# Complex products of the high tables: additions moved from VectorE to accumulating DMAs, cosine bias as a constant, half the DMA scratch

## The chip, the cores and the metric

The kernel runs on one core of a Trainium2 chip. The metric is the device time in microseconds of one execution, as a median over runs. The engines are named as in the profile: PE (TensorE matmuls) with PEld (its weight loads), DVE (VectorE), ACT (ScalarE), POOL (GpSimd) and SP (SyncE). SP, ACT and POOL can issue DMAs; those of POOL go through the software queue (q0 in the profile), those of SP and ACT through hardware queues (q1, q10).

## The reference, cut to what matters

The output joins two independent halves of 448 columns over 2048 positions, in bfloat16.

```
# half A: linear attention, 16 heads of 28
q, k, v = split(x @ wqkv)
phi(t)  = concat(softmax(t @ w_phi), softmax(-(t @ w_phi)))
o       = phi(q) @ (phi(k)^T v) / (phi(q) . sum phi(k) + 1e-6)
a       = o @ wo
# half B: state space convolution, 448 channels with 256 complex states each
dt = exp(log_dt);  A = A_re + i A_im;  B, C likewise
P[d, n, l] = exp(dt[d] A[d, n] l)              # l = 0 .. 2047, in bf16 steps
K[d, l]    = Re( sum_n C[d, n] dt[d] B[d, n] P[d, n, l] )
y          = causal convolution of u with K along l  +  u * Dskip
```

What matters here is K. The exponent is split as l = hi + lo. A table of C dt B exp(dt A hi) for 32 values of hi (the high table) and a table of exp(dt A lo) for 50 values of lo are multiplied and summed over the states by PE.

## The kernel before, in words

The 448 channels are cut into eight chunks of 56. States lie on the 128 partitions, in two halves, so that a chunk has COLS = 112 columns per table entry. For each chunk k these steps run:

- `dampings` and `rotations` (L733 to L744): PE forms the arguments in PSUM, ACT evaluates Exp into `E`, and Sin twice into `W`, once for the cosine (line L742, with pi/2 as bias) and once for the sine. Each `use` covers 224, 448 or 896 columns per instruction.
- `hi_tables` (L760): the high table `U[:, k % 2]`, 32 entries, each a real and an imaginary row of 112 columns. Entries 0 to 3 are copied from `H`; then five levels follow, each a complex product of earlier entries with a power from `PW` (128, 256, or 512 three times): entries 4-7 from 0-3, 8-15 from 0-7, 16-23 from every second one of 0-15, 24-27 from every second one of 16-23, and 28-31 from 24-27. Each level reads what the one before it wrote. The product itself is `cmul` (L605): four `tt` calls (L416 to L419) on DVE, with the scratch tile `t2`.
- `damp` (L746): DVE multiplies `W` by `E`; then the sign flip of line L757 runs on ACT (profile line L758) or DVE.
- `build_k` (L773): PE multiplies `U` by `W`, 112 small matmuls per half chunk, and a copy brings the result from PSUM into `Ts`.

`U`, `W` and `E` have two places, by the parity of k. Between the chunks the program places the key side of half A (`key_tile`, L794), its queries (`query`, L836), the spectrum of u (`signal_spectrum`, L672), and the scattering of K from `Ts` to rows of `Kt` by many small DMAs on SP, POOL and ACT (`scatter_k`, L896). After the chunks come the spectrum of K, `load_su` (L973, the spectrum of u back from DRAM), the products and the inverse transform (`conv_group`, L1015).

The order of the instructions is fixed when the program is built. `Plan` (L148) collects units of work; a unit has a cost per engine on which it may run, its reads and writes, and a rank by its step label. `Plan.run` (L214) walks a clock of its own: at each step it takes the engine that can start earliest and, among units that can start then, that of the lowest rank in `RANKS` (L105). A unit that may run on ACT or DVE goes to whichever is free first. For ACT steps with a table, `PHASES` (L141) is a second order: a phase of a higher number may not start while one of a lower number is left; even numbers are Exp, odd ones Sin. For a DMA, `dma` (L457) gives the cost of its issue and a time on the wires (`load`), from which `run` sets the moment from which readers may be placed. On the chip each engine then executes its own queue in order and waits on semaphores. All engines' working data lie in one SBUF tile, at byte offsets written out by hand (L471 on).

The four lines of the product before:

```
        tt(tmp, src, pw(1), ALU.mult)
        tt(dst, src, pw(0), ALU.mult)
        tt(d[0], d[0], t[1], ALU.subtract)
        tt(d[1], d[1], t[0], ALU.add)
```

Of the kernel before, what the change touches and what calls it, by code (L numbers as in the profile page):

```python
# [9 lines left out]
BF16 = mybir.dt.bfloat16  # L10
# [89 lines left out]
def pair_rows(x2, row, t, col):  # L100
# [4 lines left out]
RANKS = {"in": 76, "inAre": 129, "inAim": 160, "inCre": 137, "inBre": 274, "inCim": 272, "inBim": 280, "inx0": 84,  # L105
         "inx1": 209, "inx2": 217, "inx3": 227, "inqk": 141, "inG": 164, "inv_": 281, "one": 67, "pid": 139, "bd":
         124, "dt": 198, "stAre": 19, "stAim": 18, "amp": 265, "hl": 238, "cs128": 177, "cs32": 202, "cs64": 161,
         "stCre": 14, "stBre": 260, "stCim": 8, "stBim": 140, "cb": 230, "H32": 98, "H64": 35, "pw": 57, "xT0": 277,
         "xT1": 190, "xT2": 121, "xT3": 0, "fold1": 135, "fold0": 235, "vones": 49, "late0": 24, "late1": 259,
         "late2": 15, "zero": 206, "ua0.0": 147, "ab0.0": 136, "ua0.1": 143, "ab0.1": 59, "ua0.2": 123, "ab0.2": 148,  # L110
         "ua0.3": 252, "ab0.3": 88, "us0.0": 215, "us0.1": 3, "us0.2": 5, "us0.3": 30, "us0.4": 50, "us0.5": 219,
         "us0.6": 203, "us0.7": 48, "exps0": 271, "rot0": 70, "hi0.0": 42, "hi0.1": 192, "hi0.2": 46, "hi0.3": 105,
         "hi0.4": 263, "hi0.5": 196, "exps1": 257, "rot1": 183, "hi1.0": 34, "hi1.1": 81, "hi1.2": 37, "hi1.3": 110,
         "hi1.4": 158, "hi1.5": 261, "damp0": 233, "neg0": 207, "build0.0": 65, "build0.1": 255, "ua1.0": 131,
         "ab1.0": 269, "ua1.1": 16, "ab1.1": 226, "ua1.2": 248, "ab1.2": 106, "ua1.3": 78, "ab1.3": 182, "us1.0": 33,
         "us1.1": 166, "us1.2": 68, "us1.3": 262, "us1.4": 234, "us1.5": 97, "us1.6": 126, "us1.7": 1, "key0": 225,
         "key1": 80, "key2": 171, "key3": 239, "key4": 253, "key5": 167, "key6": 151, "key7": 91, "exps2": 276,
         "rot2": 77, "hi2.0": 178, "hi2.1": 61, "hi2.2": 29, "hi2.3": 279, "hi2.4": 231, "hi2.5": 111, "damp1": 211,
         "neg1": 107, "build1.0": 113, "build1.1": 28, "exps3": 201, "rot3": 208, "hi3.0": 267, "hi3.1": 174, "hi3.2":
         115, "hi3.3": 157, "hi3.4": 243, "hi3.5": 218, "damp2": 240, "neg2": 132, "build2.0": 138, "build2.1": 237,  # L120
         "key8": 216, "key9": 133, "key10": 118, "key11": 173, "key12": 89, "key13": 36, "key14": 116, "key15": 93,
         "keyend": 146, "exps4": 176, "rot4": 205, "hi4.0": 223, "hi4.1": 108, "hi4.2": 153, "hi4.3": 63, "hi4.4": 26,
         "hi4.5": 47, "damp3": 40, "neg3": 23, "build3.0": 128, "build3.1": 125, "kt5": 244, "sc0": 247, "exps5": 32,
         "rot5": 258, "hi5.0": 275, "hi5.1": 254, "hi5.2": 199, "hi5.3": 212, "hi5.4": 270, "hi5.5": 7, "damp4": 52,
         "neg4": 79, "build4.0": 200, "build4.1": 163, "qe0": 117, "qz0": 104, "q0.0": 112, "q0.1": 142, "q0.2": 222,
         "q0.3": 144, "qe1": 96, "qz1": 92, "q1.0": 11, "q1.1": 134, "q1.2": 31, "q1.3": 69, "exps6": 22, "rot6": 94,
         "hi6.0": 189, "hi6.1": 56, "hi6.2": 12, "hi6.3": 246, "hi6.4": 43, "hi6.5": 188, "damp5": 169, "neg5": 38,
         "build5.0": 159, "build5.1": 175, "sc1": 229, "exps7": 213, "rot7": 250, "hi7.0": 273, "hi7.1": 266, "hi7.2":
         85, "hi7.3": 102, "hi7.4": 120, "hi7.5": 165, "damp6": 75, "neg6": 64, "build6.0": 194, "build6.1": 181,
         "negid": 54, "gi": 101, "su0": 187, "qe2": 185, "qz2": 100, "q2.0": 152, "q2.1": 9, "q2.2": 21, "q2.3": 119,  # L130
         "qe3": 156, "qz3": 242, "q3.0": 25, "q3.1": 2, "q3.2": 122, "q3.3": 168, "f0.0": 45, "ks0.0.0": 27,
         "ks0.0.1": 55, "f0.1": 197, "ks0.1.0": 179, "ks0.1.1": 103, "f0.2": 145, "ks0.2.0": 149, "ks0.2.1": 245,
         "f0.3": 86, "ks0.3.0": 210, "ks0.3.1": 53, "f0.4": 264, "ks0.4.0": 214, "ks0.4.1": 71, "f0.5": 127,
         "ks0.5.0": 193, "ks0.5.1": 191, "f0.6": 249, "ks0.6.0": 17, "ks0.6.1": 114, "f0.7": 184, "ks0.7.0": 62,
         "ks0.7.1": 90, "damp7": 278, "neg7": 41, "build7.0": 51, "build7.1": 73, "ks1.3.0": 10, "ks1.3.1": 95,
# [231 lines left out]
def kernel(  # L367
# [62 lines left out]
    def act(out_, a, func, phase=None, scale=1.0, bias=None, n=None):  # L430
        kw = {} if bias is None else {"bias": bias}
        plan.add({"ACT": 0.055 + (n or count(out_)) * 0.833e-3 + (0.093 if bias is not None else 0)},
                 lambda: nc.scalar.activation(at(out_), at(a), func, scale=scale, **kw),  # L433
                 [whose(a)] + ([] if bias is None else [bias]), [out_], phase)
# [718 lines left out]
```

## Time and profile before

| | |
|---|---|
| time, median of 3 runs | 342.79 us (341.43 to 343.74) |
| profiled execution, span | 341.7 us (the page gives no time outside the span) |
| DVE busy | 309.2 us (90%), 438 instructions |
| PE busy | 266.8 us (78%) |
| ACT busy | 254.2 us (74%) |
| POOL busy | 54.3 us (16%), 99 instructions |
| ACT_TABLE_LOAD | 12, 1283 ns each |
| DMA | 32.88 MB, of it 4.26 MB on the software queue |

The profile is that of one execution. Busy time counts an engine's instructions without waits and without overlap; the mean duration of an instruction in a group can exceed its share of the busy time, where the next one starts before it ends. In a timeline or a chain, the columns are the start, the length of a merged piece, the engine, the line, the operation with output and input shapes (partitions x elements), and the count. A line is often that of a helper: L419 is every two-input DVE operation, L433 every activation, L443 every copy out of PSUM, L468 every DMA issue. In a group the numbers are busy us, mean ns of one, and the idle time just before with its releasers. In the list of DMAs the last number is the median time from issue to landing, which the profile gives for POOL's alone.

### The profile page before, as it was taken

How to read it: one execution, taken by the hardware profiler on the slowest of the kernel's cores; microseconds unless marked ns; L12 is line 12 of the kernel's file. 1: busy time of each engine (PE TensorE's matmuls, PEld its weight loads, DVE VectorE, ACT ScalarE, POOL GpSimd, SP SyncE). 2: the span in 40 equal slices, each digit the busy share in tenths (PEclk: the TensorE clock that was granted, in tenths of full speed). 3: DMA queues.
4: the chain of work that ended last, by engine and by line, in shares of the span. 5: the costliest groups of instructions: out<-in, count | busy, mean ns of one | idle time of the engine just before them, and what ended most of it. 6: DMA issues, size and time to landing. Idle time of an engine off the chain costs nothing. (4 is left out here: it accounts for less than half of the span.)

```text
span 341.7 us, 9894 instructions
## 1 busy us (share of the span) xinstructions
PE 266.8 (78%) x4193; PEld 210.5 (62%) x4193; DVE 309.2 (90%) x438; ACT 254.2 (74%) x466; POOL 54.3 (16%) x99
## 2 busy tenths in 40 slices
PE   2536767888585989879997869998987686959984
PEld 1435743554563854755686647787775366949984
DVE  0578999999999999998999899999997979999992
ACT  4789999995999996986899999999976112214330
POOL 2100000000000000000019500007920035910000
PEclk9965579999899999998989998999998769999999
DMA  6994111221001002100203210322539968533333
GB/s 165 236 325 102 25 54 59 82 81 54 19 30 39 31 2 82 56 2 2 84 2 28 51 57 19 109 81 12 146 95 351 352 173 166 157 112 89 102 108 111
DMA packets 31062, 32.88 MB, mean 96 GB/s; under 512 B 8603, under 2 KB 29596, under 8 KB 30634
## 3 DMA queue, kind: packets, MB, share of 16 engines
q1 hardware_dynamic: 24338, 26.79, 25.9%
q0 software_dynamic: 3568, 4.26, 5.8%
q10 hardware_dynamic: 3112, 1.19, 1.6%
q8 instruction: 33, 0.54, 0.7%
q14 instruction: 11, 0.09, 0.1%
HBM read 24.28 MB, written 7.34 MB: 93 GB/s over the span
## 5 line engine op out<-in xcount | busy, mean ns | idle before, releaser
L453 PEld LDWEIGHTS <-sbuf 128*32 128x32 bf16 (+5 forms) x4049 | 196.2, 122 | 105.3 <-issue 52.5
L419 DVE TENSOR_TENSOR sbuf<-sbuf 128x448 bf16<-128x448 bf16 (+8 forms) x291 | 239.2, 872 | 7.0 <-ACT sbuf L433 3.1
L453 PE MATMUL mm<-sbuf 128*32 128x50 bf16 (+8 forms) x2151 | 144.7, 280 | 24.7 <-DVE sbuf L419 5.7
L433 ACT ACTIVATE sbuf<-arg 128x448 bf16<-128x448 f32 (+3 forms) x152 | 89.5, 710 | 0.0
L453 PE MATMUL kb<-sbuf 128*32 128x50 bf16 (+8 forms) x1152 | 74.7, 255 | 15.3 <-DVE sbuf L419 9.6
L443 ACT CAST sbuf<-mm 128x448 bf16<-128x448 f32 (+3 forms) x71 | 41.5, 599 | 25.2 <-PE mm L453 15.6
L453 PE MATMUL arg<-sbuf 128*128 128x112 bf16 (+1 forms) x746 | 49.0, 224 | 12.2 <-ACT sbuf L433 6.8
L468 POOL DMA_DIRECT2D sbuf<-sbuf x75 | 42.4, 594 | 92.0 <-ACT sbuf L443 90.4
L433 ACT ACTIVATE sbuf<-arg,sbuf 128x448 bf16<-128x448 f32 (+2 forms) x64 | 47.2, 738 | 0.8 <-PE arg L453 0.7
L443 ACT CAST sbuf<-kb 128x448 bf16<-128x448 f32 (+4 forms) x38 | 21.4, 572 | 20.7 <-PE kb L453 17.8
L433 ACT ACTIVATE sbuf<-mm 128x448 bf16<-128x448 f32 (+1 forms) x58 | 30.4, 604 | 8.0 <-PE mm L453 7.7
L809 DVE TENSOR_REDUCE sbuf<-sbuf 128x32 f32<-128x896 bf16 x16 | 17.2, 1072 | 1.2 <-ACT sbuf L433 1.2
L433 ACT ACT_TABLE_LOAD x12 | 15.4, 1283 | 3.5 <-issue 3.3
L633 PE MATMUL kb<-sbuf 128*112 128x128 bf16 x64 | 8.7, 310 | 10.2 <-DMA sbuf<-in_A_x_dram 7.8
L443 DVE CAST sbuf<-mm 128x448 bf16<-128x448 f32 (+3 forms) x22 | 13.2, 609 | 2.4 <-PE mm L453 2.4
L443 ACT CAST sbuf<-arg 128x224 bf16<-128x224 f32 (+1 forms) x13 | 4.6, 391 | 13.8 <-PE arg L453 13.8
L633 PEld LDWEIGHTS <-sbuf 128*112 128x112 bf16 x64 | 7.8, 208 | 11.3 <-DMA sbuf<-in_A_x_dram 8.4
L758 ACT ACTIVATE sbuf<-sbuf 128x1680 bf16<-128x1680 bf16 x8 | 13.9, 1732 | 0.7 <-DVE sbuf L419 0.7
L443 DVE CAST sbuf<-kb 128x448 bf16<-128x448 f32 (+2 forms) x15 | 9.2, 618 | 3.6 <-PE kb L453 1.9
L433 ACT ACTIVATE sbuf<-sbuf 128x896 f32<-128x896 f32 (+1 forms) x11 | 11.8, 1115 | 0.0
L419 DVE TENSOR_TENSOR sbuf<-kb,sbuf 128x448 bf16<-128x448 f32 (+3 forms) x19 | 9.9, 544 | 1.9 <-PE kb L453 1.8
L419 DVE TENSOR_TENSOR sbuf<-mm,sbuf 128x448 bf16<-128x448 f32 (+1 forms) x21 | 11.3, 566 | 0.4 <-PE mm L453 0.4
(35 smaller groups left out, 81.1 us busy)
## 6 DMA issues: line engine op xcount, KB each, us to landing
sbuf<-const SPq DMA_DIRECT2D x36, 224.0 KB
SUd<-sbuf SPq DMA_DIRECT2D x16, 224.0 KB
sbuf<-const SPq DMA_DIRECT2D x3, 1024.0 KB
sbuf<-in_A_x_dram SPq DMA_DIRECT2D x4, 448.0 KB
out_dram<-sbuf SPq DMA_DIRECT2D x16, 112.0 KB
sbuf<-in_B_u_dram SPq DMA_DIRECT2D x4, 448.0 KB
sbuf<-SUd POOLq DMA_DIRECT2D x1, 1792.0 KB, 17.9
sbuf<-SUd POOLq DMA_DIRECT2D x2, 896.0 KB, 10.0
```

Source lines behind the costliest of these rows:

```text
L419: lambda: nc.vector.tensor_tensor(out=at(out_), in0=at(a), in1=at(b), op=op), [whose(a), whose(b)], [out_])
L433: lambda: nc.scalar.activation(at(out_), at(a), func, scale=scale, **kw),
L443: lambda e: (nc.scalar.copy if e == "ACT" else nc.vector.tensor_copy)(at(out_), at(a)), [whose(a)], [out_])
L453: nc.tensor.matmul(out_, lhsT=lhsT, rhs=rhs, start=start, stop=stop, **kw)
L468: plan.add({e: own[e] for e in engs}, lambda e=engs[0]: QUEUES[e].dma_start(out=out_, in_=in_), r, w, lat=lat, load=pieces / 16000 * max(2 ...
L633: mms(p, [lambda t, j=j, x=x: nc.tensor.transpose(t[:, j, :], x[:, 112 * j:112 * j + 112], ident[:, :]) for j in range(4)], 0.4, [x, ident ...
L758: lambda en: nc.scalar.mul(m, m, -1.0) if en == "ACT" else nc.vector.tensor_scalar_mul(m, m, -1.0), [m], [m])
L809: plan.add({"DVE": 0.98}, lambda: nc.vector.tensor_reduce(zk[:, :, :], EK[:, :, :].rearrange("p s (h f) -> p s h f", f=D_HEAD), axis=AX.X, ...
```

## The change

1. In `hi_tables` each level's product is written as two DVE multiplications and one DMA. The first multiplies the source, read with its real and imaginary halves swapped, by (-im, im) into `t2`. The second multiplies the source by the real part into the destination. Then a DMA issued from POOL adds `t2` to the destination, SBUF to SBUF, with the add operation of the DMA. The negated imaginary parts `nq` are made once per chunk, on ACT or DVE, for the three powers together. `t2` gets a tile per level, at three places in turn.
2. `dma` takes `add`, which passes the operation on and doubles the planned time on the wires. The planner takes 1.0 us for the issue of such a DMA.
3. The cosine's bias is the constant pi/2 instead of a column in SBUF; the DVE memset of that column is gone, and the planner counts 93 ns less for these activations.
4. The scratch in SBUF for descriptors of software DMAs is set to 8192 bytes per partition; no size was given before. The working tile grows from 212800 to 219584 bytes per partition, and some small tiles move.
5. `RANKS` and `PHASES` are new throughout.

`cmul` stays as it is for the two products `H32` and `H64` at the start. The diff, without `RANKS`, and of `PHASES` the last part:

```diff
-          18, "key14": 18, "key15": 20, "exps4": 24, "rot4": 23, "exps5": 22, "rot5": 27, "qe0": 18, "qe1": 20, "exps6":
-          34, "rot6": 35, "exps7": 28, "rot7": 35, "qe2": 28, "qe3": 28}
+         "exps4": 26, "rot4": 23, "exps5": 16, "rot5": 27, "qe0": 24, "qe1": 16, "exps6": 30, "rot6":
+         37, "exps7": 28, "rot7": 43, "qe2": 60, "qe3": 56}
...
-    sb = Bytes(sb_pool.tile([128, 212800 // 2], BF16, name="sbuf"))
+    sb = Bytes(sb_pool.tile([128, 219584 // 2], BF16, name="sbuf"))
...
-    def act(out_, a, func, phase=None, scale=1.0, bias=None, n=None):
-        kw = {} if bias is None else {"bias": bias}
-        plan.add({"ACT": 0.055 + (n or count(out_)) * 0.833e-3 + (0.093 if bias is not None else 0)},
-                 lambda: nc.scalar.activation(at(out_), at(a), func, scale=scale, **kw),
-                 [whose(a)] + ([] if bias is None else [bias]), [out_], phase)
+    def act(out_, a, func, phase=None, scale=1.0, bias=0.0, n=None):
+        plan.add({"ACT": 0.055 + (n or count(out_)) * 0.833e-3},
+                 lambda: nc.scalar.activation(at(out_), at(a), func, scale=scale, bias=bias),
+                 [whose(a)], [out_], phase)
...
-    def dma(engs, out_, in_, r=(), w=(), lat=None, cost=0.45):
+    def dma(engs, out_, in_, r=(), w=(), lat=None, cost=0.45, add=False):
...
-        plan.add({e: own[e] for e in engs}, lambda e=engs[0]: QUEUES[e].dma_start(out=out_, in_=in_), r, w, lat=lat,
-                 load=pieces / 16000 * max(28 + 0.025 * piece, 0.0407 * piece))
+        kw = {"accum_op": ALU.add} if add else {}
+        plan.add({e: own[e] for e in engs}, lambda e=engs[0]: QUEUES[e].dma_start(out=out_, in_=in_, **kw), r, w, lat=lat,
+                 load=pieces / 16000 * max(28 + 0.025 * piece, 0.0407 * piece) * (2 if add else 1))
...
-    plan.add({"DVE": 0.1}, lambda: nc.vector.memset(bias_hp[:, :], PI / 2), [], [bias_hp[:, :]])
...
-            act(rows(W[:, k % 2, 0]), src, ACT.Sin, phase, scale=f, bias=bias_hp[:, :])
+            act(rows(W[:, k % 2, 0]), src, ACT.Sin, phase, scale=f, bias=PI / 2)
...
         copy(u[:, 0:4], H[:, :, :, cols], 0.41e-3)
+        nq = sb("nq", [128, 3, COLS], BF16, oNQ, bufs=2)
+        ims = sb("PWall", [128, 3, 2, NCOL], BF16, oPW)[:, :, 1, cols]
+        plan.add({"ACT": 0.33, "DVE": 0.19}, lambda en: nc.scalar.mul(nq[:, :, :], ims, -1.0) if en == "ACT" else
+                 nc.vector.tensor_scalar_mul(nq[:, :, :], ims, -1.0), [ims], [nq[:, :, :]])
...
-            t2 = sb("t2", [128, 8, 2, COLS], BF16, oT2)
-            cmul(dst, src, lambda i: PW[j][:, i, cols].unsqueeze(1).unsqueeze(1).to_broadcast([128, n, 2, COLS]),
-                 t2[:, 0:n])
+            t2 = sb(f"t2{lv}", [128, n, 2, COLS], BF16, (oT2C, oT2, oT2B, oT2C, oT2)[lv])
+            re, im = PW[j][:, 0, cols], PW[j][:, 1, cols]
+            neg = nq[:, min(lv, 2), :]
+            both = bass.AP(tensor=neg.tensor, offset=neg.offset, ap=[neg.ap[0], [0, n], [im.offset - neg.offset, 2], [1, COLS]])
+            back = bass.AP(tensor=src.tensor, offset=src.offset + COLS, ap=[*src.ap[:2], [-COLS, 2], [1, COLS]])
+            plan.add({"DVE": 0.065 + 2 * n * COLS * 0.522e-3},
+                     lambda t2=t2, back=back, both=both: nc.vector.tensor_tensor(out=t2, in0=back, in1=both, op=ALU.mult),
+                     [src, neg, im], [t2])
+            tt(dst, src, re.unsqueeze(1).unsqueeze(1).to_broadcast([128, n, 2, COLS]), ALU.mult)
+            dma(["POOL"], dst.rearrange("p n c x -> p (n c x)"), t2.rearrange("p n c x -> p (n c x)"), r=[t2, dst], w=[dst],
+                cost=1.0, lat=1.0, add=True)
...
-    nc = _bacc.Bacc("TRN2", target_bir_lowering=False, num_devices=1)
+    nc = _bacc.Bacc("TRN2", target_bir_lowering=False, num_devices=1, dynamic_dma_scratch_size=8192)
```

## The prediction

> **What bounds the kernel now.** I read the page from the top: busy shares, the 40 slices, then the stage table, the chain that ended last, and the groups of instructions by form. The first two views of the page:
>
> ```profile
> span 341.7 us, 9894 instructions
> PE 266.8 (78%) x4193; PEld 210.5 (62%) x4193; DVE 309.2 (90%) x438; ACT 254.2 (74%) x466; POOL 54.3 (16%) x99
> ...
> DVE  0578999999999999998999899999997979999992
> ACT  4789999995999996986899999999976112214330
> ```
>
> VectorE is the fullest engine and is full in nearly every slice from the fifth on. ScalarE is nearly as full up to slice 30 (about 257 us), then mostly idle. The share of 90% hides that, so I cut the span there:
>
> ```profile
> core 0: us, PE busy (x) PEld busy (x) DVE busy (x) ACT busy (x) POOL busy (x), PEclk, DMA share, GB/s
> 0.00:40.00 40.00, 18.93 (x165) 16.82 (x166) 24.52 (x36) 30.86 (x41) 3.78 (x14) 0.74 0.66 177
> 40.00:257.00 217.00, 182.85 (x3003) 135.70 (x3002) 211.49 (x317) 199.13 (x376) 33.41 (x60) 0.95 0.19 52
> 257.00:342.00 85.00, 65.04 (x1028) 58.00 (x1027) 73.24 (x88) 24.17 (x52) 17.16 (x26) 0.91 0.57 171
> ```
>
> Three stages. The start waits for loads. In the table stage (40 to 257 us) DVE is idle 5.5 us of 217 and ACT 18. In the tail DVE works 73 of 85 us and ACT 24. All eight chunks' high tables lie between 40 and 277 us. DMA has room in the table stage: share 0.19. The chain that ended last agrees about the tail ("DVE sbuf L419 14%" of the span, the largest part), and one of its pieces is the last chunk's tables:
>
> ```profile
> 262.91 12.08 DVE sbuf L419 x15
> ```
>
> **What is removed from DVE.** Per chunk `hi_tables` makes five complex products of four `tt` each: two multiplications over n x 224 elements, a subtraction and an addition over n x 112, with n = 4, 8, 8, 4, 4. The last two of each four go: 3 x 2 instructions of 448 elements and 2 x 2 of 896, over eight chunks 48 and 32. Their price:
>
> ```profile
> L419 DVE TENSOR_TENSOR sbuf<-sbuf 128x896 bf16<-128x896 bf16 x98 | 57.5, 613 | 0.9 <-ACT sbuf L443 0.4
> ...
> L419 DVE TENSOR_TENSOR sbuf<-sbuf 128x448 bf16<-128x448 bf16 x72 | 25.2, 380 | 0.2
> ```
>
> and in the timeline of DVE
>
> ```profile
> 233.02 0.68 DVE L419 TENSOR_TENSOR sbuf<-sbuf 128x448 bf16<-128x448 bf16 x2
> ...
> 267.59 1.15 DVE L419 TENSOR_TENSOR sbuf<-sbuf 128x896 bf16<-128x896 bf16 x2
> ```
>
> The mean of one instruction (613 and 380 ns) is too much, since neighbours overlap: two of 896 take 1.15 us, so the step from start to start is 1.15 - 0.61 = 0.54; two of 448 take 0.68, a step of 0.30. Removed: 48 x 0.30 + 32 x 0.54 = 31.7 us, nearly all in the stage where DVE has no gaps. The two multiplications per level stay; the one for `t2` reads its source with the halves swapped and a factor laid out as (-im, im), but the same number of elements with contiguous runs of 112, so I leave its time as it is.
>
> **What is added to DVE or ACT.** One multiplication by -1 over 336 elements per chunk (`nq`). On DVE it lies between the 128-element one (195 ns) and the 896-element bf16 copy (345 ns): about 0.24 us, eight times 1.9 us. On ACT it lies between 349 and 541 ns (copies of 224 and 448). I take DVE, the dearer for the bound. The deleted `bias_hp` memset (about 0.1 us) was in the start, where DVE waits: nothing. Net on DVE so far: -29.8 us.
>
> **The cosine bias.** 64 rotation activations read `bias_hp`, and so do three at the start, which wait for loads anyway.
>
> ```profile
> 236.06 0.66 ACT L433 ACTIVATE sbuf<-arg,sbuf 128x448 bf16<-128x448 f32 x1
> 236.58 0.56 ACT L433 ACTIVATE sbuf<-arg 128x448 bf16<-128x448 f32 x1
> 237.01 0.48 ACT L433 ACTIVATE sbuf<-arg,sbuf 128x224 bf16<-128x224 f32 x1
> 237.34 0.39 ACT L433 ACTIVATE sbuf<-arg 128x224 bf16<-128x224 f32 x1
> ```
>
> The starts show the occupied time: 0.52 us with the operand, 0.43 without; the smaller pair gives 0.33 and 0.23. So 0.09 us each, 64 x 0.09 = 6 us of ACT; if the constant were passed as an operand after all, nothing. The Trainium skill, page "ScalarE: Activation LUTs" (What ACT_TABLE_LOAD costs), says that each per-partition pointer operand adds about 93 ns; the starts agree, while the group means (728 against 679 ns) show only 49 and would make 3 us of it. By the new PHASES the sequence of Exp and Sin steps changes kind once more, since queries 2 and 3 (60 and 56) now follow the last rotation (43): one more ACT_TABLE_LOAD of 1283 ns. Net on ACT -4.7 us.
>
> **The 40 accumulating DMAs, the unknown price.** Each is issued by POOL, waits for both multiplications and ends before the next level may read. POOL is busy 54 us; 40 issues at 0.59 (row "L468 POOL DMA_DIRECT2D sbuf<-sbuf", 594 ns) to 1.7 us (load of SUd, 1714 ns) add 24 to 68 us, which fits in the span. They move 128 rows of 1792 or 3584 bytes, 224 or 448 KB, 12.8 MB in all; the hardware queue moved 26.79 MB in 25.9% of the span, 3.3 us a MB, so 42 us of wire time, 84 if an accumulation counts twice, in a stage with 175 us free.
>
> What matters is issue to landing. From below, the 56 KB loads issued by POOL landed after 2.1 us; from above, 896 KB landed after 10.0:
>
> ```profile
> sbuf<-SUd POOLq DMA_DIRECT2D x2, 896.0 KB, 10.0
> ...
> sbuf<-in_B_u_dram POOLq DMA_DIRECT2D x4, 56.0 KB, 2.1
> ```
>
> Taking 2.1 us plus 3.3 us a MB once or twice gives 2.8 to 3.5 us for 224 KB and 3.5 to 4.9 for 448. By the line between those two rows it is 3.7 and 5.8, and with the data counted twice 5.3 and 9.5. I take 3.5 and 4.9, nearest to the POOL loads of long rows. The planner's code reserves 3.0 and 4.2 us, and that sets the order of the queues: it puts other work on DVE for that long. Five levels in a row take 3 x 3.5 + 2 x 4.9 = 20.3 us of DMA, plus 3 x 1.15 + 2 x 2.08 = 7.6 us of multiplications: 28 us per chunk. Tables are double buffered and a chunk now takes 217 / 8 = 27 us, so a table may start almost two periods ahead; the chain itself doesn't limit the rate. At the long prices, 3 x 5.3 + 2 x 9.5 + 7.6 = 43 us, it still would not.
>
> What does cost is DVE's queue, which is in order: where a level lands later than planned, everything behind it waits, key tiles, damping products and PSUM copies, then PE (through PSUM buffers), then ACT. POOL's queue is in order too: the scattering of K, 75 issues in bursts of up to 25 (14 us), stands in the same queue, and a level behind such a burst is late by it. Excess over plan is 0.5 and 0.7 us, 2.9 us per chunk, 23 us over eight if no slack covers any of it. In the table stage DVE's waits sum to 5.5 us now, since each result is ready before its turn; with five spread levels per chunk most of the excess meets such slack. I take 5 us; the ends are 0 and the full 23.
>
> The swapped-over work: ACT can hand the sign flip at L758 (8 x 1.73 us) to DVE at about 0.5 us each (by the two short rows above), 4 us on DVE for 14 off ACT. I count these 4 us, because in a shorter table stage ACT (199 - 5 over less than 200 us) would otherwise be the next limit. Queries 2 and 3 move 16 Exps (8 us) out of that stage too, into the tail where ACT is idle; their DVE work only changes place.
>
> Smaller scratch and moved buffers: three `t2` places instead of one remove write-after-read waits between levels; the trace shows none of them as a wait, so nothing. With a smaller descriptor ring the second of the two 896 KB loads may have to wait for the first, between 0 and its 10 us, and the scatter behind it on POOL comes 6 us later now: 0 to 4 us late for the last group's spectrum. I take 0 and leave the 4 to the range.
>
> **The sum.** DVE busy 309.2 - 29.8 + 4 = 283.4. DVE idles 32.5 us now (15.5 in the start, 5.5 in the table stage, the rest in the tail); I keep that and add 5. Span 321. The profiled execution's span is 341.7; the page gives no time outside it, and the median is 342.8, 1.1 more. So 321 + 1 = 322 us.
>
> **Rivals.**
> - *Another engine takes over.* If the sign flips stay on ACT and PSUM copies do not move, ACT in the table stage is 199.1 - 4.7 - 8 = 186 plus its 18 us of idling: 204 instead of 217, a gain of 13, so 330. PE speaks for it as well: 183 of 217 us. Against it: ACT has 61 us idle in the tail and copies are planned onto either engine.
> - *Slower: the levels stall DVE's queue.* Waits per chunk are 20.3 us, 162 us in all. DVE gains 25.8 net, so the change loses once more than 16% of that is exposed, 0.65 us per level. With a third exposed: 342.8 - 25.8 + 54 = 371; with a quarter, 357, which I take. For it: today these products run back to back and DVE needs no DMA at all; the long price of 9.5 us is not excluded. Against: of each period of 27 us the products' own multiplications take 7.6, so DVE has other work for 70% of it. The Trainium skill, page "DMA: Bandwidth & Descriptors" (Anatomy of one DMA), puts the fixed part of a software DMA at about 2 us plus bytes over 436 GB/s, by which the levels are 2.5 and 3.1 us (an estimate) and the waits 110 us. The 56 KB row agrees with the fixed part; no row of this trace shows an accumulation.
> - *Nothing comes of it.* If the tail hangs on the last rotation, which ACT ends at 257 us, and ACT's saving is only the 4.7 us with the stalls as taken: 343, no change.
>
> **Chances.** Forecast (312 to 328) 0.48; another engine takes over (326 to 339) 0.22; stalled queue (347 to 375) 0.23; nothing 0.07. About 1% is what a measurement of this kernel can tell from no change. Faster by more than 1%: 0.70; within 1%: 0.07; slower: 0.23. The range of 8 in 10 goes from 310 to 354: it leaves out most of the stalled cases and little below, where only stalls of zero together with copies moved to ACT would lead.
>
> **What would show it.** Right: L419 has 80 instructions fewer; DVE busy near 283 with the same share or more; 40 POOL issues of 224 and 448 KB landing within 5 us; DVE waits for "DMA sbuf<-sbuf" of a few us in total; starts of cosine activations 0.43 apart. Wrong: such DVE waits above 25 us, landing above 6 us, POOL issues much longer than 1 us, or ACT idle under 8 us in a table stage that is still over 205 us long.

## The result, and the profile after

The changed kernel takes 375.48 us (median, 373.8 to 376.84), the kernel before in the same comparison 343.03 (341.43 to 343.74): ratio 1.0946, interval 1.0906 to 1.0987. The forecast was 322, its range ended at 354. The change makes the kernel 9.5% slower, by 32.4 us. A time here is the median of all executions of a kernel; the ratios leave out those more than 1.5% above its fastest, and the traces of `f1` (349.8 us) and `f3` (345.9 us) below are of such slow executions.

The page of the kernel after, its head and two of the slices:

```profile
span 374.7 us, 9944 instructions
...
PE 271.0 (72%) x4193; PEld 215.1 (57%) x4193; DVE 290.9 (78%) x376; ACT 242.1 (65%) x456; POOL 82.3 (22%) x127
...
DVE  1699998987777987888258997997795789917792
ACT  3999986895996698969867899796111221323420
```

VectorE and ScalarE both have less to do, by 18.3 and 12.1 us, and yet the span is 33 us longer. Neither is full any more: the row of nines of DVE is gone, and ACT is idle more often in the table stage. The stages of the kernel after, cut where ACT turns idle:

```profile
40.00:272.00 232.00, 175.42 (x2850) 129.46 (x2850) 188.11 (x251) 184.37 (x355) 65.12 (x92) 0.90 0.46 98
272.00:375.00 103.00, 74.63 (x1148) 66.91 (x1144) 74.22 (x93) 24.69 (x54) 13.34 (x22) 0.89 0.55 155
```

Columns as before (stage, length, busy PE, PEld, DVE, ACT, POOL, clock, DMA share). The table stage has grown from 217 to 232 us, with DVE idle 44 us in it instead of 5.5, and ACT 48 instead of 18. The tail has grown from 85 to 103: the last chunk's tables ended 20 us into it before and end 39 us into it now. What DVE waits for, in us, times and the longest:

```profile
DVE sbuf L779 <- DMA sbuf<-sbuf: 22.6, 17, 6.0
DVE sbuf L419 <- ACT sbuf L442: 13.4, 4, 8.6
...
DVE sbuf L419 <- DMA sbuf<-sbuf: 4.9, 4, 2.7
```

L779 is the swapped multiplication of the next level. 27.5 us of DVE's waits are for the new DMAs; before there were none. The DMAs themselves, KB each and median us from issue to landing:

```profile
sbuf<-sbuf POOLq DMA_DIRECT2D x16, 448.0 KB, 4.7
sbuf<-sbuf POOLq DMA_DIRECT2D x24, 224.0 KB, 3.3
```

These medians are close to the 4.9 and 3.5 us of the prediction. POOL was busy 0.84 to 0.97 us for nearly every one. But the landings of all 40, added up from the trace, are 188 us, where the prediction's prices make 16 x 4.9 + 24 x 3.5 = 162 and the times that the planner reserved make 16 x 4.2 + 24 x 3.0 = 139. The 26 us between 188 and 162 are in five DMAs that landed after more than 6 us, among them two in flight together (6.8 and 7.0) and one at 17.6.

So the price was near, and the sign was wrong. Three accounts were open. **The order**: the new order of the queues, spread out for the landings, gives away DVE's gain. **The landings**: results come later than their place in DVE's queue, at 0.7 us per level. **Another engine**: less DVE work is worth little, because ScalarE is nearly as full. The planner's order changes entirely with any change of its inputs, so all experiments keep the order of the kernel after (or of the kernel before) and change only what a step emits.

### The profile page after: what moved, and what is told of

Same layout as the page of the kernel before. It is cut to its first block, busy times and chain, and to the rows that moved or that the text cites. A ratio compares the mean times of both kernels' runs of the same rounds, so it can differ in the third digit from the quotient of the medians.

```text
span 374.7 us, 9944 instructions
## 1 busy us (share of the span) xinstructions
PE 271.0 (72%) x4193; PEld 215.1 (57%) x4193; DVE 290.9 (78%) x376; ACT 242.1 (65%) x456; POOL 82.3 (22%) x127
## 5 line engine op out<-in xcount | busy, mean ns | idle before, releaser
L452 PEld LDWEIGHTS <-sbuf 128*32 128x32 bf16 (+5 forms) x4049 | 200.6, 123 | 138.4 <-issue 85.0
L419 DVE TENSOR_TENSOR sbuf<-sbuf 128x896 bf16<-128x896 bf16 (+11 forms) x171 | 177.1, 1078 | 26.5 <-ACT sbuf L442 13.4
L468 POOL DMA_DIRECT2D sbuf<-sbuf x104 | 71.9, 808 | 184.8 <-DVE sbuf L419 123.8
L432 ACT ACTIVATE sbuf<-arg 128x448 bf16<-128x448 f32 (+3 forms) x216 | 107.2, 632 | 6.1 <-DVE sbuf L419 5.0
L452 PE MATMUL kb<-sbuf 128*32 128x50 bf16 (+7 forms) x1214 | 77.3, 263 | 20.2 <-DVE sbuf L419 10.4
L442 ACT CAST sbuf<-mm 128x448 bf16<-128x448 f32 (+4 forms) x65 | 34.4, 540 | 51.2 <-PE mm L452 38.2
L779 DVE TENSOR_TENSOR sbuf<-sbuf 128x896 bf16<-128x896 bf16 (+1 forms) x40 | 31.9, 807 | 22.8 <-DMA sbuf<-sbuf 22.6
L442 ACT CAST sbuf<-kb 128x448 bf16<-128x448 f32 (+4 forms) x33 | 17.2, 535 | 34.2 <-PE kb L452 20.6
L442 DVE CAST sbuf<-mm 128x448 bf16<-128x448 f32 (+2 forms) x35 | 21.6, 626 | 14.0 <-PE mm L452 9.5
L432 ACT ACTIVATE sbuf<-mm 128x448 bf16<-128x448 f32 (+1 forms) x54 | 27.5, 593 | 7.2 <-PE mm L452 7.1
L821 DVE TENSOR_REDUCE sbuf<-sbuf 128x32 f32<-128x896 bf16 x16 | 17.1, 1078 | 2.1 <-ACT sbuf L432 2.0
L432 ACT ACTIVATE sbuf<-sbuf 128x896 f32<-128x896 f32 (+1 forms) x11 | 11.6, 1118 | 0.0
L419 DVE TENSOR_TENSOR sbuf<-kb,sbuf 128x448 bf16<-128x448 f32 (+2 forms) x20 | 11.0, 572 | 0.0
L758 ACT ACTIVATE sbuf<-sbuf 128x1680 bf16<-128x1680 bf16 x5 | 8.0, 1607 | 2.7 <-DVE sbuf L419 2.7
## 6 DMA issues: line engine op xcount, KB each, us to landing
sbuf<-SUd POOLq DMA_DIRECT2D x1, 1792.0 KB, 18.3
```

Of the source, the lines that this page charges most:

```text
L419: lambda: nc.vector.tensor_tensor(out=at(out_), in0=at(a), in1=at(b), op=op), [whose(a), whose(b)], [out_])
L442: lambda e: (nc.scalar.copy if e == "ACT" else nc.vector.tensor_copy)(at(out_), at(a)), [whose(a)], [out_])
L452: nc.tensor.matmul(out_, lhsT=lhsT, rhs=rhs, start=start, stop=stop, **kw)
L468: plan.add({e: own[e] for e in engs}, lambda e=engs[0]: QUEUES[e].dma_start(out=out_, in_=in_, **kw), r, w, lat=lat, load=pieces / 16000 * ...
L758: lambda en: nc.scalar.mul(m, m, -1.0) if en == "ACT" else nc.vector.tensor_scalar_mul(m, m, -1.0), [m], [m])
L779: lambda t2=t2, back=back, both=both: nc.vector.tensor_tensor(out=t2, in0=back, in1=both, op=ALU.mult),
```

## The experiments

### The DMAs left out, and made by VectorE

`e1_no_add` is the kernel after without the 40 DMAs; the sums are made nowhere. `e2_add_on_dve` puts one DVE addition in the place of each.

```diff
-    lambda e=engs[0]: QUEUES[e].dma_start(out=out_, in_=in_, **kw)
+    lambda e=engs[0]: None if add else QUEUES[e].dma_start(out=out_, in_=in_)                                    # e1
+    lambda e=engs[0]: nc.vector.tensor_tensor(out=out_, in0=out_, in1=in_, op=ALU.add) if add else QUEUES[e]...  # e2
```

> The kernel after with the 40 additions left out altogether (entries 4 to 31 of the high tables lack the crossed part), every queue otherwise in the order of the kernel after. Theory L (the five levels of a chunk and the chunks themselves follow one another, and each level waits for a DMA of 3.2 to 4.2 us and more, so the DMA's time to landing sets the pace of the table stage): without the DMAs the 27.5 us of DVE waits on them go and the order closes up, 330 to 348 us. Theory O (the new order of the queues, with queries 2 and 3 behind the tables and other ranks, is by itself poor, whoever adds): above 362 us. Theory S (the smaller descriptor ring or the software queue's other DMAs hold POOL): no large gain, above 362 us, with POOL late at the scattering of K.

> The kernel after with each accumulating DMA replaced by one VectorE addition over the same elements (896 or 1792), put at the same place in the order; nq, the swapped multiplication, the constant bias, the scratch size and the order of all else stay. It adds 24 x 0.54 + 16 x 1.00 = 29 us of DVE work and takes every DMA wait out of the product. Theory L: 345 to 360 us, faster than the 375 of the kernel after although DVE has more to do. Theory O: 370 us or more, since the order is the same and DVE has 29 us more work.

Measured: e1 348.36 us, ratio to before 1.0161 (1.0105 to 1.0217); e2 360.03, 1.0514 (1.0449 to 1.0579). Both lie just above the upper edge of what theory L gave, and below the 362 and 370 of the others. The DMAs cost 375.5 - 348.4 = 27 us, in sum as much as DVE's 27.5 us of waits for them. The other finding weighs more: without any addition, by DMA or DVE, the kernel is still no faster than before. From the page and the waits of e1:

```profile
PE 268.7 (78%) x4193; PEld 213.3 (62%) x4193; DVE 288.6 (83%) x376; ACT 240.6 (69%) x456; POOL 46.5 (13%) x87
```

```profile
DVE sbuf L442 <- PE mm L452: 8.6, 10, 2.3
DVE sbuf L419 <- ACT sbuf L442: 8.0, 5, 2.8
DVE sbuf L419 <- ACT sbuf L432: 6.2, 8, 1.6
```

DVE has 20.6 us less to do than before and spends them waiting for PE and ACT. In the kernel before, its wait for activations (L433 there, L432 here) was 3.1 us.

### Which part of the landing, and where

`e6_plain_copy` drops the add operation: `t2` overwrites the destination, so the sum is left out. `e5_two_dmas` makes each accumulation in two halves. `e7_last_chunk_no_add` leaves the five additions of chunk 7 out, `e8_only_last_chunk_adds` those of the other seven. `e4_load_on_sp` issues the 1792 KB load of `SUd` from SP instead of POOL.

```diff
-    ...dma_start(out=out_, in_=in_, **kw)
+    ...dma_start(out=out_, in_=in_)                                                    # e6
+    for o, i in ((out_[:, :m], in_[:, :m]), (out_[:, m:], in_[:, m:])) if add else ((out_, in_),):
+        QUEUES[e].dma_start(out=o, in_=i, **kw)                                        # e5
+    skip = add and plan.now.startswith("hi7")                                          # e7; e8: add and not ...
+    ... skip or QUEUES[e].dma_start(out=out_, in_=in_, **kw)
-            w=[SUs[gi]], cost=1.7)
+            w=[SUs[gi]], cost=1.7, on="SP" if gi == 0 else None)                       # e4
```

> The kernel after with the 40 transfers as plain copies (t2 overwrites the destination; the sum is left out, so the output is not the reference's). Theory: the landing time of 3.1 to 3.3 us (224 KB) and 4.2 us (448 KB) is that of a transfer from SBUF to SBUF issued by POOL, and adding costs it little: copies land within 0.2 us of that and the time is within 1% of 375. Rival: the reading and adding at the destination is what makes them slow: copies land in under 2.7 and 3.5 us, and since five landings stand in a row in each of eight chunks (0.5 to 0.7 us each, 23 us in all) the time falls to 355 to 368.

> The kernel after with each accumulating DMA issued as two of half the length, in the same place. POOL takes 0.85 us more per level, and a level's sum is complete about 0.4 to 0.9 us later. Theory L (the chain of levels sets the pace): 40 x 0.4 to 40 x 0.9, 16 to 36 us more, 391 to 411 us. Theory O (the order costs, the DMAs' time has slack): within 4 us of 375.

> The kernel after, order kept, with the five additions of the last chunk left out (they are not made anywhere, so the output is not the reference's). The last halves of build 6 and build 7 start 50 us apart in the kernel after, 26 us in the kernel before, and 41 us with no additions at all. Theory: DVE's waits on transfers are lost all along the eight chunks (22.8 us of the 27.5 us lie ahead of 250 us, 4.7 us behind), so this gives 4 to 9 us: 366 to 371. Rival: the last chunk, with its transfers among the big loads, carries most of the loss, as the 50 us suggest: 13 to 22 us, 353 to 362.

> The counterpart: the kernel after, order kept, with the additions of chunks 0 to 6 left out and only those of the last chunk made by accumulating DMAs (the output is not the reference's). Theory: the seven chunks' waits go, 18 to 23 us: 352 to 357. Rival, with most of the loss in the last chunk: 5 to 14 us, 361 to 370.

> The kernel after with the 1792 KB load of u's spectrum issued by SP instead of POOL, all else in the same order. In the kernel after the second level of the last chunk's table is issued by POOL 3.3 us behind this load and lands after 17.6 us, where the others of its size take 4.2 to 5.7. Theory Q (it waits in the software queue behind the load): it lands within 8 us and the time falls by 8 to 13 us, to 362 to 367. Theory W (it waits for the wires, which the load fills whoever issues it): it lands after 12 us or more and the time changes by less than 4 us.

| run | us | ratio to before | against 375.5 |
|---|---|---|---|
| e6, plain copies | 357.56 | 1.0402 (1.0349 to 1.0454) | -18 |
| e5, in two halves | 386.2 | 1.1254 (1.1225 to 1.1284) | +11 |
| e7, chunk 7 without | 365.73 | 1.0664 (1.0605 to 1.0723) | -10 |
| e8, only chunk 7 with | 358.36 | 1.0435 (1.0381 to 1.0488) | -17 |
| e4, big load on SP | 374.8 | 1.0954 (1.0886 to 1.1021) | -1 |

e5 falls between its two theories. For e6 the theory on record fell and its rival held. The rows of the copies, and what is left of DVE's wait:

```profile
sbuf<-sbuf POOLq DMA_DIRECT2D x16, 448.0 KB, 3.3
sbuf<-sbuf POOLq DMA_DIRECT2D x24, 224.0 KB, 2.5
```

```profile
DVE sbuf L779 <- DMA sbuf<-sbuf: 8.9, 7, 5.4
```

Adding at the destination costs 0.8 us on 224 KB and 1.4 us on 448 KB, and the issue on POOL 0.85 us instead of 0.54. The Trainium skill, page "DMA: Bandwidth & Descriptors" (Anatomy of one DMA), gives 2.0 us plus bytes over 436 GB/s, an estimate of 2.5 and 3.1 us here: the copies of e6 agree (2.5 and 3.3), the accumulations of the kernel after do not (3.3 and 4.7).

The landings of e6 add up to 139 us, by chance just what the planner reserved. The sums agree, not each landing: the medians are 0.5 and 0.9 us under plan, and one took 14.4 us. So e6 shows roughly what the kernel would take if the plan's prices had been met: 357.6 us, still 4% over before. From e1 to e6, 139 us of landing cost 9.2 us of time; from e6 to the kernel after, 49 us more cost 17.9, over a third of them. That is what one would see if time that the order had allowed for is mostly hidden and time beyond it much less; since the single landings differ from the plan, it is not proved.

e7 and e8 divide the 27 us: 9.8 for the last chunk's five, 17.1 for the other 35, together 26.9. The cost is thus additive, 0.5 us per DMA in the first seven chunks and 2.0 in the last. e7 lies just below the theory's band and e8 1.4 us above it: most is lost all along the chunks, but the last one costs more than its waits of DVE (4.7 us) told. Its second level met the big load. POOL's timeline in the kernel after:

```profile
266.14 1.73 POOL L468 DMA_DIRECT2D sbuf<-SUd  x1 [6.43 <-PE kb L452]
269.48 0.87 POOL L468 DMA_DIRECT2D sbuf<-sbuf  x1 [1.61 <-DVE sbuf L419]
289.54 0.85 POOL L468 DMA_DIRECT2D sbuf<-sbuf  x1 [19.19 <-DVE sbuf L419]
```

The line at 269.48 is that level; it landed after 17.6 us, the 1792 KB load ahead of it after 18.3, and the next level was issued 20 us later. But DVE itself, on its way to the next multiplication, waited only 3.1 us for that landing:

```profile
287.14 1.09 DVE L779 TENSOR_TENSOR sbuf<-sbuf 128x1792 bf16<-128x1792 bf16 x1 [3.08 <-DMA sbuf<-sbuf]
```

In e4, with the load on SP, the same level landed after 8.2 us, and the time did not change. POOL, and DVE's multiplication, in e4:

```profile
270.42 0.88 POOL L468 DMA_DIRECT2D sbuf<-sbuf  x1 [10.25 <-DVE sbuf L419]
287.03 0.85 POOL L468 DMA_DIRECT2D sbuf<-sbuf  x1 [15.73 <-DVE sbuf L419]
```

```profile
284.65 1.08 DVE L779 TENSOR_TENSOR sbuf<-sbuf 128x1792 bf16<-128x1792 bf16 x1
```

The next issue still waits 15.7 us for a DVE multiplication, although its input had landed at 278.6. In both kernels DVE's queue has the same other work between the two levels, about 13 us of copies and products, and reaches the multiplication at 284. So an earlier landing could give back the 3.1 us at most, and part of those went at once: the third operation after this multiplication now waited 2.1 us instead of 0.7 for a load of u. Of the two theories, W had the time right and neither had the landing right. The most visible wait of POOL's timeline was not worth a microsecond, because POOL is not the engine that is short of time.

### The old order

These kernels have before's order, the product in the form of the kernel after (swapped multiplication, `nq` made with the chunk's first copy), its buffer places and its ring. `c_none_one_add` makes each sum by one DVE addition, `c_last_level` by a DMA for the last level of each chunk (8 DMAs), `c_all_old_order` by DMA throughout.

```diff
-            cmul(dst, src, ..., t2[:, 0:n])
+            nc.vector.tensor_tensor(out=own, in0=back, in1=both, op=ALU.mult)
+            tt(dst, src, re..., ALU.mult)
+            if lv in LEVELS:                       # (), (4,), (0, 1, 2, 3, 4)
+                nc.gpsimd.dma_start(out=a, in_=b, accum_op=ALU.add)
+            else:
+                nc.vector.tensor_tensor(out=a, in0=a, in1=b, op=ALU.add)
```

> The same kernel as in the run with DMAs in the old order, but each product's two additions are one DVE addition over both halves (swapped multiplication and nq as in the change, constant bias, smaller scratch, no accumulating DMA). DVE: 40 instructions fewer, about 0.07 us each, 2.8 us, against at most 1.9 us for nq; ACT 6 us less. All theories: 340 to 343.5 us. If the swapped multiplication were slower than a plain one, or the smaller scratch cost something, above 345 us.

> As the run with one addition on DVE, but the last level of each chunk, which only PE's builds read, adds by an accumulating DMA: 8 of 40. Theory L: no later level waits for it, so DVE loses 8 x 0.54 = 4.3 us of work and waits for none of these DMAs; PE's builds start up to 3 us later where they follow at once, and PE has gaps: 336 to 340 us, 2 to 5 us below the run with none. Theory P (the DMA itself disturbs, through POOL or SBUF): no gain, 341 us or more.

> The kernel before, with its own order of every queue (the planner still counts two DVE operations), in which the two additions of each of the 40 products are replaced by one accumulating DMA from POOL, as in the change; constant bias, smaller scratch and three t2 places too. Theory L (a level's DMA stands between it and the next one, and DVE's queue in order passes that on): in this order a chunk's levels stand close together, so most of the 20 us per chunk is exposed: 8 x 10 to 8 x 16 us more, 31 us of DVE work less, 390 to 440 us. Theory O (the new order costs the time, not the DMAs): below 375 us, the time of the kernel after.

Measured: 351.56 us (ratio 1.025, 1.0208 to 1.0291), 373.08 (1.0878, 1.0831 to 1.0925) and 434.27 (1.265, 1.2602 to 1.2698). Against no additions at all (f1 below, 347.2 us), 40 DMAs cost 87 us in the old order, 2.2 us per level, as theory L gave, and 27 us in the new one. The new order does its work: it hides 86% of 188 us. DVE's wait in the kernel with all 40:

```profile
DVE sbuf L786 <- DMA sbuf<-sbuf: 103.6, 27, 11.6
```

With eight only, at the end of each chunk, the kernel is 21.5 us slower than with none, where theory L had it 2 to 5 us faster. PE now waits for five of the eight DMAs. PE's waits in `c_last_level`, and POOL's timeline ahead of two of the DMAs (L793):

```profile
PE mm L453 <- DMA sbuf<-sbuf: 30.1, 5, 17.3
```

```profile
247.70 9.63 POOL L468 DMA_DIRECT2D sbuf<-sbuf  x16 [16.88 <-ACT sbuf L443]
257.27 1.07 POOL L793 DMA_DIRECT2D sbuf<-sbuf  x1
...
289.71 1.71 POOL L468 DMA_DIRECT2D sbuf<-SUd  x1 [16.75 <-DVE sbuf L795]
297.63 1.69 POOL L468 DMA_DIRECT2D sbuf<-SUd  x1 [6.20 <-issue]
299.31 0.94 POOL L793 DMA_DIRECT2D sbuf<-sbuf  x1
```

The first stands behind a burst of 16 scattering DMAs, the second behind two loads of the spectrum: POOL issued them 4.3 and 8.5 us after their multiplications had ended. PE waited 1.2 and 17.3 us for these two; the other three of the five were issued within a microsecond, and PE waited 11.6 us for their landings.

### The small parts

`e3_bias_alone` is the kernel before with the constant bias, `d_scratch_alone` with the smaller ring, `f2_flips_on_dve` is `c_none_one_add` with the sign flips of `nq` always on DVE.

```diff
-        kw = {} if bias is None else {"bias": bias}
+        kw = {} if bias is None else {"bias": PI / 2}                                    # e3
-    nc = _bacc.Bacc("TRN2", target_bir_lowering=False, num_devices=1)
+    nc = _bacc.Bacc("TRN2", target_bir_lowering=False, num_devices=1, dynamic_dma_scratch_size=8192)   # d_scratch
-            (nc.scalar.mul if e == "ACT" else nc.vector.tensor_scalar_mul)(nq[:, :, :], ims, -1.0)
+            nc.vector.tensor_scalar_mul(nq[:, :, :], ims, -1.0)                          # f2
```

> The kernel before with the constant as the cosine's bias and nothing else changed; the order of all queues is that of the kernel before. ACT is occupied about 0.09 us less for each of 64 activations, 6 us. If ACT's queue is a limit of the table stage: 337 to 340 us. If DVE alone is: 342 to 343 us, no difference to be measured. It isn't slower under any theory; if it is, the constant costs something that the rows don't show.

> The kernel before with the smaller DMA scratch (8192 bytes) alone. Theory: the smaller ring lets the second 896 KB load of the spectra leave only when the first is through (7 us later, as the run with before's order and one DVE addition showed) and the scatter behind it on POOL is pushed out: 2 to 7 us slower, 345 to 350. Rival: there is slack behind these loads and the ring costs nothing: 341 to 344, ratio 1.00 within its interval. Then the 9 us of that run come from something else, the new sign flips and their waits on ACT.

> The run with before's order and one DVE addition per product (351.6 us), with all eight sign flips of the powers on DVE instead of on the engine of the first copy (most on ScalarE there). Theory: the first multiplication of a chunk waited for ScalarE's flip, and with the flip on DVE itself at 0.2 us the time goes back to before's: 342 to 346. Rival: the flips are not the cause: 349 to 353, and what made that run 9 us slower stays with the one long addition in place of two halves, or with where the buffers lie.

e3: 342.55 us, ratio 0.9973 (0.9934 to 1.0012), no difference, though ACT's busy time falls from 254.2 to 249.8. d_scratch: 343.25, 1.0013 (0.9979 to 1.0047): no difference either, though the ring does hold a load back. POOL in the kernel with the smaller ring; before, both loads went out together at 276.0:

```profile
273.53 1.72 POOL L468 DMA_DIRECT2D sbuf<-SUd  x1 [17.88 <-DVE sbuf L419]
282.39 1.69 POOL L468 DMA_DIRECT2D sbuf<-SUd  x1 [7.14 <-issue]
```

f2: 348.38, 1.0154 (1.0113 to 1.0195), between the two expectations: the flips on ACT are some 3 us of the 9 by which `c_none_one_add` lost. The expectation for `c_none_one_add`, 340 to 343.5 us, was missed by 8 us. The remaining 5 us, from one long addition in place of two halves, from the buffers' places, or from the ring in that company, are not explained.

### Is VectorE's time worth anything?

`f1_old_order_no_add` is `c_none_one_add` with the additions left out (made nowhere). `f3_old_order_no_add_no_flip` leaves out the eight sign flips of the rotations as well, which run on ACT; `f4_before_no_flip` leaves those out of the kernel before, and nothing else. `f5_flips_on_pool` and `f6_flips_on_dve` are complete kernels: before with the constant bias, and the rotations' flips on POOL or on DVE.

```diff
-                    nc.vector.tensor_tensor(out=a, in0=a, in1=b, op=ALU.add)
+                    pass                                                             # f1, f3
-                 lambda en: nc.scalar.mul(m, m, -1.0) if en == "ACT" else nc.vector.tensor_scalar_mul(m, m, -1.0)
+                 lambda en: None                                                      # f3, f4
+                 lambda en: nc.gpsimd.tensor_scalar_mul(m, m, -1.0)                   # f5; f6: nc.vector
```

> Before's order with the two multiplications of each product as in the kernel after, sign flips of the powers on the engine of the chunk's first copy, constant bias, and the 40 additions left out (made nowhere, so the output is not the reference's). DVE loses the same 31 us as in the kernel after without additions, which took 348 us in the new order; with one DVE addition per product the old order took 351.6, the new one 360. Theory: in an order that isn't spread out for landings the DVE work taken away shortens the run: 318 to 330. Rival: in the old order too something else holds the table stage as soon as DVE is lighter (ScalarE's 183 to 199 us of 217, or the sign flips), and the order is not what cost the gain: 338 to 350.

> Before's order without the 40 additions, and also without the eight sign flips of the rotations (the multiplication of 1680 elements by -1, 13 us of ScalarE's busy time; both are made nowhere, so the output is not the reference's). Without the additions alone it took 347 us, although DVE had 31 us less: its waits were for ScalarE's activations. Theory: ScalarE is as full as VectorE and takes over at once, so that only both together shorten the table stage: 330 to 338. Rival: neither is the bound; the stage hangs on waits between queues whose order is fixed: 344 to 349.

> The kernel before without the eight sign flips of the rotations (13 us of ScalarE's work; made nowhere, so the output is not the reference's), VectorE's work as it was. Theory, VectorE and ScalarE equally full: ScalarE's relief alone brings little, 339 to 344. Rival, ScalarE alone is the bound: 328 to 336.

> The kernel before, complete and in its order, with the constant bias, and the eight sign flips of the rotations done by POOL (GpSimd) instead of ScalarE. Left out altogether the flips are worth 0.5% (341.6 against 343.7). Theory, both engines equally full: ScalarE is relieved of 13 us and VectorE isn't loaded, so at most those 0.5%: 341 to 344. Rival: the flip takes POOL long (several us for 1680 elements) and the build of K waits for it: 346 to 355.

> The kernel before, complete and in its order, with the constant bias, and the eight sign flips of the rotations done by VectorE at 0.6 us instead of ScalarE at 1.7. ScalarE loses 14 us, VectorE gains 5. Theory, both engines equally full: no gain or a small loss, 342 to 346. Rival, ScalarE alone sets the stage: 336 to 340.

| before's order | DVE busy | ACT busy | us | ratio to before |
|---|---|---|---|---|
| c_none, one DVE addition | 308.9 | 251.4 | 351.56 | 1.025 (1.0208 to 1.0291) |
| f1, no addition | 281.3 | 251.5 | 347.2 | 1.011 (1.0074 to 1.0146) |
| f3, no addition, no flips | 281.0 | 239.8 | 337.3 | 0.9807 (0.9763 to 0.9852) |
| f4, before without flips | 308.8 | 243.6 | 341.56 | 0.9954 (0.9919 to 0.999) |
| f6, before, flips on DVE | 312.6 | 239.0 | 344.76 | 1.0037 (1.0002 to 1.0071) |
| f5, before, flips on POOL | 328.8 | 238.7 | 362.89 | 1.0554 (1.0505 to 1.0604) |

f1 came out as its rival said, f3, f4 and f6 as their theories did, and f5 8 us above even its rival's range. f1 decides between the order and the other engine: in the old order too, 27.6 us less DVE work bring 4.4 us, and in the new order 27.8 us bring 11.7 (e2 to e1). The new order has a price of its own: with the additions on DVE it takes 360.0 us and the old one 351.6. But the account by which it gives the gain away falls: without additions the new order takes 348.4 and the old one 347.2. The table stage of f1, and three of DVE's waits:

```profile
40.00:257.00 217.00, 182.61 (x2759) 131.98 (x2757) 179.21 (x235) 190.12 (x365) 31.93 (x60) 0.90 0.18 48
```

```profile
DVE sbuf L419 <- ACT sbuf L433: 9.7, 11, 1.8
DVE sbuf L443 <- PE mm L453: 7.5, 6, 2.5
DVE sbuf L837 <- ACT sbuf L433: 6.6, 6, 2.6
```

DVE is now idle 38 of the 217 us in which it had been idle 5.5. Added up over this stage, it waits 17.1 us for ACT and 16.4 for PE, where before it was 1.6 and 1.3; in e1, in its own table stage, it is 11.6 and 13.3. Then the flips: taken off ACT while DVE is full they are worth 2 us (f4), with DVE light 10 us (f1 to f3; the two pairs also differ in the form of the product). So DVE and ACT limit together, and relieving one of them brings a small part. PE may be a third limit: it is busy 183 of the 217 us both before and in f1, and no run gave it less to do. Shifting work from ACT to DVE gains nothing (f6), and POOL is no help (f5): one flip takes it 4.8 us, and it slows DVE down. But together the additions and the flips are 39 us of busy time and bring 14 (c_none to f3), so two busy engines are not the whole story either. What holds the rest is not settled; PE, or waits from queue to queue in an order that stays fixed, are guesses that no run tested. No complete version was faster than before by more than the noise.

## Why the prediction was wrong, step by step

- **The failed step** is the sum: "DVE busy 309.2 - 29.8 + 4 = 283.4. DVE idles 32.5 us now [...] I keep that and add 5." It keeps VectorE's idle time, so that a microsecond off its busy time is a microsecond off the kernel. The work did go: 40 additions are 27.8 us of DVE (e2 against e1), and the kernel after has 290.9 (11 more copies on DVE, 7.3 us, are the bulk of the difference). But DVE's idle time over the span, 32.5 us before, is 57.8 in e1, which has no DMA to wait for, and 83.8 in the kernel after, where the sum had 37.5. Taken away alone, DVE's work is worth 4 us in the old order (c_none to f1) and 12 in the new one (e2 to e1). The idle time grows as the busy time falls, because DVE then waits for results of other engines: ACT's, as the flips show, and PE's, which no run relieved. The view that hinted at it was on the page: ACT 199 and PE 183 of 217 us.
- **"Another engine takes over" (330)** had the right engine, ScalarE, and too much hope. Its gain of 13 us came from the bias and the Exps that leave ACT's table stage, with ACT's idling there kept at 18 us. In e1 ACT is busy 185 us in that stage, near the 186 reckoned (though three of eight flips, 595 ns each on DVE where 0.5 was expected, and 11 copies had moved to DVE), but it is idle 37, and no gain is left.
- **The landing price** was right in the median and low in the sum: 188 us against 162. The excess over the plan was 49 us and not 23; the 26 us more are those of the five DMAs that landed after more than 6 us.
- **"I take 5 us; the ends are 0 and the full 23."** The landings cost 27. The plan's own 139 us, counted as hidden for nothing, cost about 9 (e6), the 49 beyond it about 18. "A few us in total" of DVE's waits for these DMAs were 27.5, above the 25 that the text named as the sign of a wrong forecast.
- **"Slower: the levels stall DVE's queue"** is what happened, at 27 us exposed. That is about the 25.8 us at which the landings would eat DVE's gain, 16% of the 162 us it reckoned (14% of the 188 measured), and below the quarter it took. On its own terms the kernel would have come out even; it lost 32 us because the gain set against the stall wasn't there. The two rivals were priced apart; each leans on the other's part going well, and they came together: 343, plus the 5 by which e1 exceeds before, plus 27 for the DMAs, is 375.
- **"The chain itself doesn't limit the rate"** is not contradicted, nor shown: second levels of successive chunks were issued 25 to 31 us apart (the last pair 42), about its 28 us, but copies with shorter landings kept the same order, and a kernel with chains made independent was not tried.
- **Right**: issues on POOL of 0.84 to 0.97 us, a 13th table load, the swapped multiplication at the price of the plain one (1083 ns for 1792 elements in `c_none_one_add`, 1082 before), the bias at a few us of ACT (4.4 in e3, 6 expected) and nothing of the time, the ring at nothing. That the moved buffers cost nothing is not shown: they are among the causes that the 5 us of `c_none_one_add` may have.

## What to carry to other kernels

The busiest engine's time is not the length of the kernel where a second engine is nearly as full in the same stage: before counting a saving, look at what the next engines allow in that stage, and take the saving out alone to see what it brings. A transfer put into a chain of dependent steps costs a part of what it lands beyond its planned place, here about a third, and a smaller part of the rest; price it with what it will meet on its queue, not by a transfer alone, and look at what the waiting engine would do meanwhile. Two risks that each leave a gain standing can have no gain left together, so the case in which both come true needs a price of its own.

## What the runs showed of the hardware

- An accumulating DMA from SBUF to SBUF lands later than a plain copy of the same size: 3.3 against 2.5 us for 224 KB, 4.7 against 3.3 for 448 KB, with 0.85 against 0.54 us of POOL for the issue. Two halves are no cure: 3.1 us for 112 KB, and the kernel takes 11 us more.
- An accumulating DMA of 448 KB behind a 1792 KB load on the same software queue landed after 17.6 us, with the load on SP after 8.2.
- With 8192 bytes of scratch the second of two 896 KB loads was issued 8.9 us after the first, with the default 1.7; the time of that kernel did not change.
- POOL as a helper of DVE. The flip of 1680 elements takes it 4790 ns (DVE 595, ACT 1732), and DVE's own instructions grow. Groups of `f5_flips_on_pool`, where before had 1082 and 4109 ns:

```profile
L419 DVE TENSOR_TENSOR sbuf<-sbuf 128x1792 bf16<-128x1792 bf16 x58 | 67.9, 1208 | 0.6 <-ACT sbuf L443 0.2
...
L419 DVE TENSOR_TENSOR sbuf<-sbuf 128x7616 bf16<-128x7616 bf16 x8 | 38.5, 4807 | 0.0
```

DVE's busy time is 328.8 us there, 20 more than before. That fits what the Trainium skill, page "GPSIMD Engine Reference" (Specifications), says: GpSimd's interfaces to SBUF are shared with VectorE, with contention for instructions that have two SBUF inputs.
